# Banded attention with a split-float32 MLP on one core: a longer run of zero matmuls at the start, and the planner's constants set anew

## The chip, the core and the metric

The kernel runs on one core of one Trainium2 chip. Five engines work side by side and wait for one another through semaphores: TensorE (PE in the profile, its weight loads PEld), VectorE (DVE), ScalarE (ACT), GpSimd (POOL) and SyncE (SP, which here issues nearly all transfers). The metric is the device time of one execution in microseconds (us), the median of several executions.

## The reference

Attention for 4 batches and 8 heads, 768 positions of 64 values, then a two-layer MLP on all 3072 tokens. A position sees the first `n_sink` = 4 positions and the last `window` = 128:

```python
keep = is_sink | in_window            # pos < n_sink; 0 <= i - j < window
scores = np.where(keep, q @ k.T / 8, -1e9)
a = softmax(scores)
x = (a @ v) as rows of 512            # 3072 x 512
h = x @ w_in                          # 512 -> 2048
g = h * np.tanh(np.log1p(np.exp(h)))
out = g @ w_out                       # 2048 -> 512
```

The sums are in float64 (the weights arrive as 64-bit numbers); the kernel's products use single precision, each operand of the MLP as a rounded part and a rest.

## The kernel before

The 12 chunks of 256 tokens (`T`) are worked in an order that takes the first chunk of each batch ahead (`c3 == 0`: no earlier keys). For each chunk and each pair of heads there is a score product (L410, or L413 where a chunk has earlier keys), a masked minimum on DVE (L427), an exponential on ACT (L430), transposes on PE (L459, L471) that are copied out of PSUM (`copy_ways`, L271 on ACT or L274 on DVE), and the product with the values (L527). The result x is held as a rounded part (a copy, L271 or L274) and a rest (a subtraction, L282 on POOL or L284 on DVE).

Each of the 16 slices of `w_in` and of `w_out` arrives as 64-bit numbers in a `raw` tile (three of them) and is turned into a rounded part and a rest by `weights`: the high word is scaled (L313 on ACT or L314 on DVE), shifted (L316, DVE) and given its sign (L317, DVE), the low word is scaled (L320 on ACT or L321 on DVE), both are added (L324 on POOL, or line 325 on DVE), then copied (L271, L274) and subtracted (L282, L284).

The MLP goes in steps of two slices. The first product is L584 for the first three chunks, L580 and L581 for the next seven, L642 for the last two, which are worked together; the activation is a chain of five operations between ACT and DVE (L593 to L598, L645 to L650), and the second product is L614 (L668 for the last two chunks). The first three chunks (`GROUP`) are interleaved, two steps each, while their weights are still being turned.

The order of the instructions on every engine is not written by hand. `Plan.solve` puts each operation on one of the engines that can do it, at the time that its own costs and waits give, and `emit` writes the operations by those times. What it weighs are the numbers at the head of the file: ranks (`LEADG` for the attention of the first three chunks, `PACE` between pairs of heads, `WA`, `WB`, `WO` for the weights, `OTF`, `OVF`, `OTP`, `OVP`, `SPL` within a pair), penalties (`PEN_C` for a copy on DVE, `PEN_W` for scaling a weight's word on DVE, `PEN_J` for adding the words on DVE, `PEN_N` for norms on ACT), and the times at which the first loads are planned to land (`EARLY`, `LINE0`). Before `COLD` a PE operation is planned at twice its time. Where the plan leaves PE without work, `emit` fills the hole with matmuls of zeros (L786), 224 columns each.

Ahead of the plan, `body` issues the first eleven loads, computes the masks, and runs `WARM` matmuls of zeros (L1027). After number `AHEAD`, counted from zero, it puts one small matmul (L1032) that spreads the two limits over the partitions. Then every engine reads a flag (L1040) and branches into the planned program.

Of the kernel before, what the change touches and what calls it, by code (L numbers as in the profile page):

```python
# [12 lines left out]
F32 = mybir.dt.float32  # L13
BF16 = mybir.dt.bfloat16
F32R = mybir.dt.float32r
I32 = mybir.dt.int32
# [5 lines left out]
B, H, S, D = 4, 8, 768, 64  # L22
DM, DF = 512, 2048
P = 128
NBLK = S // P
SK = 16
PITCH = P + SK
# [4 lines left out]
TB = 2  # L32
T = TB * P
# [10 lines left out]
       POOL: {PE: 203, ACT: 75, DVE: 80, POOL: 102}, SP: {}}  # L44
W2 = 2 * P + SK
WM = SK + P
PEN_C, PEN_S, PEN_N, PEN_J, PEN_W = 147, 0, 239, 268, 58
OTP, OVP = 1.2, 1
OTF, OVF, PACE = 1.089, 0.601, 1.542
WA, WB, WO = 1.203, -1.766, 0.423  # L50
GROUP, PART, SPARED = 3, 2, 20
PITCHN = 7
LEAD, LEADG, LEADN = 11, (54.195, 35.033, 35.128), 9
WARM, AHEAD, COLD, SPARE, ROOM = 10, 5, 2500, 250, 4
ZERO = 224
SPL = 1.5
LINE0, LINE, SLOW = 8400, 4.5, .2
EARLY = {"ks": ([P, 2 * PITCH], F32, (0, 400, 2400)), "qh": ([P, T], F32, (0, 800, 2700)),
         "vq": ([P, 2, TB, 4, D], F32, (1800, 3900)), "raw": ([P, 512, 2], I32, (4800, 6400, 9300))}
SH, QUICK = 1.0, 2  # L60
HALF = 120
SLACK, STEADY = 800, 24
# [181 lines left out]
class Fast(Base):  # L244
# [9 lines left out]
    def tile(self, b, name):  # L254
        if b.tag in EARLY:
            assert b.place == self.c.order.get(id(b), b.place), "the first loads are out of order"
            b.t = self.c.first[b.tag][b.place]
            return
        n, psum = self.TAGS[b.tag]
        tag, n = (f"{b.tag}{b.place}", 1) if b.tag in ("w", "att") else (b.tag, n)  # L260
        b.t = (self.ps if psum else self.sb).tile(b.shape, b.dtype, name=name, tag=tag, bufs=n)
# [26 lines left out]
    def load(self, prio, buf, dst, src, kb, **kw):  # L288
        if self.c.early.get(buf.tag, 0):
            self.c.early[buf.tag] -= 1  # L290
            k = len(self.c.first[buf.tag]) - self.c.early[buf.tag]
            self.c.order[id(buf)] = k - 1
            return self.plan.add(prio, {SP: (1, lambda: None, EARLY[buf.tag][2][k - 1])}, new=[buf], **kw)
        return self.transfer(prio, dst, src, kb, new=[buf], **kw)
# [58 lines left out]
    def halves(self, b, j0, i0, w, pr, rank):  # L353
# [10 lines left out]
        def twice(buf, t, src, kb):  # L364
            one = self.load(rank, buf, lambda: t()[up], heads(src), kb)
            return [one, self.transfer(rank + .01, lambda: t()[low], heads(src), kb, bufs=[buf])]
        half = lambda: f32(kr.t.rearrange("p n t -> p (n t)")[:, 0:2 * w]).rearrange("p (e w) -> p e w", e=2)
        ldk = twice(kr, half, self.k[b, pr, :, j0 * PITCH:j0 * PITCH + w], w / 2)
        ldq = twice(qr, lambda: qr.t, self.q[b, pr, :, i0 * P:i0 * P + T], T / 2)
        r = rank + SPL  # L370
        k = []
# [616 lines left out]
def body(tc, q, k, v, vs, w_in, w_out, limits, out):  # L988
    nc = tc.nc
    with ExitStack() as ctx:  # L990
        top = ctx.enter_context(tc.tile_pool(name="top", bufs=1))
        held = {tag: [top.tile(shape, dtype, name=f"{tag}{i}") for i in range(Fast.TAGS[tag][0])] for tag, (shape, dtype, _) in EARLY.items()}
        one = top.tile([1, 4], I32, name="lim_one")
# [101 lines left out]
```

## Time and profile before

| | us |
|---|---|
| median of 3 executions | 684.91 (684.52 to 685.14) |
| the profiled execution | 686.47 |
| its span, first to last instruction | 684.7 |
| PE busy | 677.2 (99%) |
| ACT busy, DVE busy, POOL busy | 536.3, 533.5, 153.1 |

The page says that PE is busy 99% of the span, but a matmul that stands and waits is drawn as busy, so this number does not tell where PE works and where it waits. The table of stretches gives more: ACT's busy time of each stretch shows where ACT has no idle left.

### The profile page before, as it was taken

The page shows a single profiled execution, that of the slowest core. Times are in us where ns is not written, and L with a number is a line of the kernel's source. Part 1 is how long each engine was busy: PE and PEld are TensorE (multiplying, and loading weights), DVE is VectorE, ACT ScalarE, POOL GpSimd, SP SyncE. Part 2 cuts the span into 40 slices and gives each one's busy share as a digit, 9 for nine tenths or more (in the row PEclk, how much of TensorE's full clock was granted, in tenths as well). Part 3 has the DMA queues.
Part 4 walks back from the last instruction along what each step waited for, and adds up shares of the span by engine and source line. Part 5 has one row for each costly group of instructions (what it writes and reads, how often), then busy time and mean ns, then how long its engine had stood idle before and what let it go on. Part 6 is the DMA issues. An engine that isn't in the chain of part 4 may idle for free.

```text
span 684.7 us, 13366 instructions
## 1 busy us (share of the span) xinstructions
PE 677.2 (99%) x4642; PEld 573.4 (84%) x4642; DVE 533.5 (78%) x1540; ACT 536.3 (78%) x1219; POOL 153.1 (22%) x144
## 2 busy tenths in 40 slices
PE   9999999999999999999999999999999999999996
PEld 5678888898888888888888888888888888888885
DVE  6998989874798988898899898888988887433333
ACT  5999999887788878777877868986886886656662
POOL 3564333411023223032222124121221210000000
PEclk9999999999999999999999999999999999999998
DMA  7555443421364145053134224234432220000001
GB/s 222 184 187 190 140 162 117 150 66 42 102 176 140 41 144 159 16 173 119 55 114 154 90 75 143 98 96 124 130 96 61 100 73 7 2 32 0 1 0 67
DMA packets 40287, 69.26 MB, mean 101 GB/s; under 512 B 4242, under 2 KB 29074, under 8 KB 40210
## 3 DMA queue, kind: packets, MB, share of 16 engines
q1 hardware_dynamic: 40064, 68.17, 31.8%
q8 instruction: 39, 0.64, 0.4%
q14 instruction: 38, 0.31, 0.1%
q10 hardware_dynamic: 146, 0.13, 0.1%
HBM read 62.00 MB, written 6.29 MB: 100 GB/s over the span
## 4 chain that ended last, share of the span: by engine, by line
PE 95%; ACT 3%; POOL 0%; DVE 0%; issue 0%; DVEq 0%; POOLq 0%
PE acc L614 31%; PE hp L580 15%; PE hp L584 9%; PE hp L581 8%; PE att L527 7%; PE att L413 5%; PE acc L668 3%; PE hp L642 3%; PE att L668 3%; PE att L642 3%; PE att L410 3%; PE att L471 2%; PE att L459 2%; ACT w L271 1%; PE att L508 1%; ACT w L313 1%
## 5 line engine op out<-in xcount | busy, mean ns | idle before, releaser
L614 PE MATMUL acc<-w,gh 128*128 128x512 f32 x640 | 166.0, 396 | 0.0
L580 PE MATMUL hp<-w,w 128*128 128x512 f32 x448 | 163.3, 400 | 0.0
L614 PEld LDWEIGHTS acc<-w,gh 128*128 128x128 f32 x640 | 113.4, 188 | 21.7 <-ACT n L271 0.2
L581 PE MATMUL hp<-w,w 128*128 128x256 f32 x448 | 125.4, 280 | 0.0
L580 PEld LDWEIGHTS hp<-w,w 128*128 128x128 f32 x448 | 84.2, 188 | 17.8 <-DVE n L590 0.3
L430 ACT ACTIVATE p<-p,nm 128x144 f32<-128x144 f32 (+2 forms) x192 | 81.0, 426 | 12.9 <-DVE nm L427 12.0
L282 POOL TENSOR_TENSOR w<-raw,w 64x416 fp32r<-64x416 f32 x41 | 44.2, 1085 | 200.3 <-ACT w L271 59.5
L614 PE MATMUL acc<-w,gl 128*128 128x512 f32 x320 | 87.1, 391 | 0.0
L581 PEld LDWEIGHTS hp<-w,w 128*128 128x128 f32 x448 | 84.5, 189 | 2.0
L590 DVE TENSOR_REDUCE n<-hp 128x256 f32<-128x512 f32 x112 | 76.7, 686 | 10.8 <-PE hp L581 9.5
L584 PE MATMUL hp<-w,w 128*128 128x256 f32 x576 | 77.6, 286 | 0.3 <-DVE u L598 0.2
L584 PEld LDWEIGHTS hp<-w,w 128*128 128x128 f32 x576 | 73.0, 191 | 4.8 <-issue 1.0
L614 PEld LDWEIGHTS acc<-w,gl 128*128 128x128 f32 x320 | 59.7, 188 | 12.8 <-issue 0.2
L271 ACT ACTIVATE gh<-n 128x512 fp32r<-128x512 f32 x69 | 43.5, 631 | 32.5 <-DVE n L598 19.4
L595 ACT ACTIVATE u<-u,bias 128x512 f32<-128x512 f32 x80 | 57.5, 719 | 11.3 <-DVE u L594 10.6
L324 POOL TENSOR_TENSOR w<-w,w 128x512 int32<-128x512 int32 x32 | 41.4, 1303 | 86.6 <-DVE w L316 29.3
L596 ACT ACTIVATE u<-u,bias 128x512 f32<-128x512 f32 x80 | 57.6, 720 | 1.3
L284 DVE TENSOR_TENSOR gl<-n,gh 128x512 fp32r<-128x512 f32 x49 | 34.3, 700 | 27.1 <-PE acc L668 24.0
L598 DVE SCALAR_TENSOR_TENSOR n<-u,n 128x512 f32<-128x512 f32 x56 | 39.7, 710 | 15.5 <-ACT u L597 15.0
L597 ACT ACTIVATE u<-u 128x512 f32<-128x512 f32 x80 | 50.1, 626 | 1.0
L593 ACT ACTIVATE u<-n 128x512 f32<-128x512 f32 x56 | 35.1, 626 | 16.6 <-DVE n L590 14.7
L527 PE MATMUL att<-pth,vq 128*64 128x64 f32 (+2 forms) x1152 | 47.8, 238 | 0.0
(135 smaller groups left out, 1227.6 us busy)
## 6 DMA issues: line engine op xcount, KB each, us to landing
vq<-v_s SPq DMA_DIRECT2D x32, 512.0 KB, 4.0
raw<-k_p SPq DMA_DIRECT2D x64, 208.0 KB, 3.5
raw<-w_in SPq DMA_DIRECT2D x16, 512.0 KB, 3.9
raw<-w_out SPq DMA_DIRECT2D x16, 512.0 KB, 3.9
w<-q_p SPq DMA_DIRECT2D x64, 128.0 KB, 3.1
y<-u SPq DMA_DIRECT2D x20, 256.0 KB, 2.0
ks<-k_p SPq DMA_DIRECT2D x16, 136.0 KB, 3.2
qh<-q_p SPq DMA_DIRECT2D x16, 128.0 KB, 3.0
```

The lines of the kernel that those rows point to most:

```text
L271: ways[ACT] = act_t(n, psum) + more, lambda: nc.scalar.activation(dst(), src(), AF.Copy, scale=scale or 1.0)
L282: ways[POOL] = pool_t(n) + more, lambda: nc.gpsimd.tensor_tensor(dst(), a(), b(), ALU.subtract)
L430: a = add(r + .05 + .01 * e, {ACT: (act_t(n, ptr=2), lambda pv=pv, nm=nm, sm=sm, j=j: nc.scalar.activation(pv(), pv(), AF.Exp, bias=nm.t[: ...
L527: yield nc.tensor.matmul(o.t[e * D:(e + 1) * D, g, o0:o1], w_, pth.t[:, e, c0:c1], start=n_ == 0, stop=n_ == len(jobs) - 1)
L580: yield nc.tensor.matmul(hp.t, wih[f].t[:, fs], xt, start=kt == 0, stop=False)
L581: yield nc.tensor.matmul(hp.t[:, 0, :], wil[f].t[:, fs], xt[:, 0, :], start=False, stop=kt == KT - 1)
L584: yield nc.tensor.matmul(hp.t[:, y, :], w_.t[:, fs], xt[:, z, :], start=kt == 0 and n_ == 0, stop=kt == KT - 1 and n_ == 2)
L590: hs.append(add(r + .3 + .1 * y, {DVE: (dve_t(2 * T), lambda y=y, hp=hp: nc.vector.tensor_reduce(m.t[:, y, :], hp.t.rearrange("p z t -> p ...
L595: a = add(r + .52, {ACT: (act_t(N, ptr=1), lambda: nc.scalar.activation(u.t, u.t, AF.Square, bias=self.one))}, [a], [u])
L596: a = add(r + .53, {ACT: (act_t(N, ptr=1), lambda: nc.scalar.activation(u.t, u.t, AF.Ln, bias=self.half, scale=0.5))}, [a], [u])
L597: a = add(r + .54, {ACT: (act_t(N), lambda: nc.scalar.activation(u.t, u.t, AF.Exp, scale=-1.0))}, [a], [u])
L614: yield nc.tensor.matmul(acc[t].t, g_.t[:, y, ts_], w_.t, start=new and n_ == 0, stop=done)
```

## The change

The zero matmuls ahead of the branch become 15 instead of 10, with the limits' matmul behind the fifth instead of the sixth. The planned landings of the first loads become 400 to 700 ns earlier, the time planned at half speed ends at 2000 instead of 2500 ns, and ranks, penalties and the room rule for the buffers (`ROOM`) get other values.

```diff
-PEN_C, PEN_S, PEN_N, PEN_J, PEN_W = 147, 0, 239, 268, 58
-OTP, OVP = 1.2, 1
-OTF, OVF, PACE = 1.089, 0.601, 1.542
-WA, WB, WO = 1.203, -1.766, 0.423
+PEN_C, PEN_S, PEN_N, PEN_J, PEN_W = 100.000, 0, 283.598, 31.148, 200.107
+OTP, OVP = 1.337, 2.737
+OTF, OVF, PACE = 0.859, 0.242, 0.879
+WA, WB, WO = 0.951, -0.426, 0.866
-LEAD, LEADG, LEADN = 11, (54.195, 35.033, 35.128), 9
-WARM, AHEAD, COLD, SPARE, ROOM = 10, 5, 2500, 250, 4
+LEAD, LEADG, LEADN = 11, (63.148, 36.967, 22.231), 9
+WARM, AHEAD, COLD, SPARE, ROOM = 15, 4, 2000, 250, 2
-SPL = 1.5
-LINE0, LINE, SLOW = 8400, 4.5, .2
+SPL = 0.723
+LINE0, LINE, SLOW = 7700, 4.5, .2
```

(`EARLY` goes the same way: the planned landings of `ks`, `qh`, `vq` and `raw` are 400 to 700 ns earlier, none below zero.)

All products stay; what moves is the order, and which engine does what. Over the whole program the counts change so:

| operation | before | after |
|---|---|---|
| L1027 zero matmuls ahead of the branch, PE | 10 | 15 |
| L786 zero matmuls in the plan's holes, PE | 14 | 37 |
| L313, L314 high word scaled on ACT, on DVE | 27, 5 | 31, 1 |
| L320, L321 low word scaled on ACT, on DVE | 26, 6 | 32, 0 |
| L324, line 325 words added on POOL, on DVE | 32, 0 | 17, 15 |
| L282, L284 rests on POOL, on DVE | 93, 180 | 120, 153 |
| L271, L274 and L273 copies on ACT, on DVE | 353, 60 | 362, 49 |

The start of the planned program on PE. `att` are score and transpose tiles, `ks` and `qh` the keys and queries of a pair of heads, `p` the exponentials, `acc<-zero` a filling matmul. Before:

```order
L410 MATMUL att_0_183<-ks_58,qh_61 128x128
L410 MATMUL att_1_184<-ks_58,qh_61 128x128
L786 LDWEIGHTS zero
L786 MATMUL acc_181<-zero 128x224
L410 MATMUL att_0_188<-ks_58,qh_61 128x256
L410 MATMUL att_1_189<-ks_58,qh_61 128x256
L459 MATMUL att_0_200<-ident,p_14_0_193 128x128 x2
```

And now:

```order
L410 MATMUL att_0_188<-ks_58,qh_61 128x128
L410 MATMUL att_1_189<-ks_58,qh_61 128x128
L786 LDWEIGHTS zero
L786 MATMUL acc_186<-zero 128x224
L410 MATMUL att_0_193<-ks_59,qh_62 128x128
L410 MATMUL att_1_194<-ks_59,qh_62 128x128
L410 MATMUL att_0_205<-ks_58,qh_61 128x256
L410 MATMUL att_1_206<-ks_58,qh_61 128x256
L459 MATMUL att_0_215<-ident,p_14_0_198 128x128 x2
```

The second pair's first scores moved ahead of the first pair's second block and of the first transposes.

The start of the planned program on ACT: `pth` are the transposed exponentials, `raw` a slice of weights, `w` a buffer for weights or x. Before:

```order
L430 ACTIVATE p_14_0_193,sm_2_195<-p_14_0_193,nm_1_194 128x128 x2
L271 ACTIVATE pth_0_205<-att_0_200 128x2x128
L430 ACTIVATE p_14_0_193,sm_2_195<-p_14_0_193,nm_1_194 128x256 x2
L430 ACTIVATE p_28_0_221,sm_2_223<-p_28_0_221,nm_1_222 128x128 x2
L313 ACTIVATE w_0_238<-raw_66 128x512
L271 ACTIVATE pth_0_205<-att_0_229 128x2x256
L430 ACTIVATE p_28_0_221,sm_2_223<-p_28_0_221,nm_1_222 128x256 x2
L271 ACTIVATE n_0_246<-att_0_258 128x256
```

And now:

```order
L430 ACTIVATE p_14_0_198,sm_2_200<-p_14_0_198,nm_1_199 128x128 x2
L430 ACTIVATE p_19_0_209,sm_2_211<-p_19_0_209,nm_1_210 128x128 x2
L271 ACTIVATE pth_0_222<-att_0_215 128x2x128
L430 ACTIVATE p_14_0_198,sm_2_200<-p_14_0_198,nm_1_199 128x256 x2
L271 ACTIVATE pth_0_240<-att_0_233 128x2x128
L320 ACTIVATE w_0_244<-raw_66 128x512
L271 ACTIVATE pth_0_222<-att_0_246 128x2x256
L271 ACTIVATE n_0_265<-rc_0_242 128x256
```

Two exponentials of the second pair moved ahead of the first copy out of PSUM, and a copy more stands ahead of the first work on a weight.

The second activation chain of the MLP on ACT (`u` is its tile, `hp` the first product). Before:

```order
L320 ACTIVATE w_0_962<-raw_68 128x512
L313 ACTIVATE w_0_971<-raw_66 128x512
L593 ACTIVATE u_0_979<-hp_0_749 128x512
L595 ACTIVATE u_0_979<-u_0_979,bias 128x512
L596 ACTIVATE u_0_979<-u_0_979,bias 128x512
```

And now:

```order
L593 ACTIVATE u_0_970<-hp_0_769 128x512
L271 ACTIVATE n_0_952<-att_0_965 128x256
L271 ACTIVATE w_0_981<-w_0_862 128x512
L271 ACTIVATE n_0_991<-rc_0_977 128x256
L271 ACTIVATE pth_0_935<-att_0_984 128x2x256
L271 ACTIVATE w_0_1006<-n_0_952 128x256
L595 ACTIVATE u_0_970<-u_0_970,bias 128x512
```

Five copies came between the chain's first and second operation on ACT, which stood next to each other before.

## Rows read from the trace of the kernel before

**Rows 1.** The profile page's line of busy times (share of the span, instructions).

```profile
PE 677.2 (99%) x4642; PEld 573.4 (84%) x4642; DVE 533.5 (78%) x1540; ACT 536.3 (78%) x1219; POOL 153.1 (22%) x144
```

**Rows 2.** Busy time by stretch: length, each engine's busy us (instructions), granted clock, DMA.

```profile
5.41:16.05 10.64, 10.64 (x49) 6.11 (x51) 5.91 (x30) 7.31 (x27) 2.39 (x3) 1.00 0.76 249
16.05:54.00 37.95, 37.89 (x287) 26.26 (x286) 34.73 (x141) 37.95 (x129) 21.55 (x22) 1.00 0.61 194
54.00:60.00 6.00, 6.00 (x45) 5.06 (x44) 5.04 (x12) 5.44 (x12) 1.75 (x2) 1.00 0.61 190
60.00:106.00 46.00, 45.92 (x298) 39.83 (x298) 41.21 (x102) 45.74 (x96) 17.76 (x14) 1.00 0.46 153
200.00:600.00 400.00, 399.98 (x3005) 345.33 (x3004) 343.50 (x1031) 315.52 (x734) 86.85 (x74) 1.00 0.31 96
```

**Rows 3.** PE in order of time: start, us, line, tiles, shape, [idle before <-releaser].

```profile
1.11 1.30 PE L1027 MATMUL busy<-zero 128*128 128x224 bf16 x6 [1.11 <-DVE zero L1011]
2.34 0.58 PE L1032 MATMUL spread<-lim,ones 1*128 1x2 f32 x2
2.86 0.93 PE L1027 MATMUL busy<-zero 128*128 128x224 bf16 x4
3.91 0.35 PE L786 MATMUL acc<-zero 128*128 128x224 bf16 x1
4.18 0.80 PE L410 MATMUL att<-ks,qh 64*128 64x128 f32 x4
...
6.85 0.58 PE L786 MATMUL acc<-zero 128*128 128x224 bf16 x2
...
12.15 1.55 PE L527 MATMUL att<-pth,vq 128*64 128x256 f32 x8
13.63 1.12 PE L459 MATMUL att<-ident,p 128*128 128x128 f32 x4
...
15.89 0.87 PE L527 MATMUL att<-pth,vq 128*64 128x256 f32 x8
...
17.48 0.66 PE L459 MATMUL att<-ident,p 128*128 128x128 f32 x4
...
24.70 0.35 PE L786 MATMUL acc<-zero 128*128 128x224 bf16 x2
```

**Rows 4.** ACT in order of time, its first operation and its waits up to 16 us.

```profile
5.41 0.40 ACT L430 ACTIVATE p<-p,nm 128x128 f32<-128x128 f32 x1 [2.76 <-DVE nm L427]
...
7.10 0.38 ACT L271 ACTIVATE pth<-att 128x256 f32<-128x256 f32 x1 [0.81 <-PE att L459]
...
10.27 0.66 ACT L313 ACTIVATE w<-raw 128x512 f32<-128x512 f32 x1 [0.86 <-DMA raw<-w_in]
...
14.30 0.42 ACT L271 ACTIVATE w<-n 128x256 fp32r<-128x256 f32 x1 [0.64 <-DVE n L534]
...
16.05 0.38 ACT L271 ACTIVATE n<-att 128x256 f32<-128x256 f32 x1 [0.95 <-PE att L508]
```

**Rows 5.** ACT in order of time, around the second activation chain and behind it.

```profile
56.58 0.60 ACT L593 ACTIVATE u<-hp 128x512 f32<-128x512 f32 x1
57.67 0.73 ACT L595 ACTIVATE u<-u,bias 128x512 f32<-128x512 f32 x1 [0.49 <-DVE u L594]
...
61.63 0.62 ACT L271 ACTIVATE w<-w 128x512 fp32r<-128x512 f32 x1
62.15 0.66 ACT L313 ACTIVATE w<-raw 128x512 f32<-128x512 f32 x1
62.72 0.66 ACT L320 ACTIVATE w<-raw 128x512 int32<-128x512 uint32 x1
63.29 0.71 ACT L595 ACTIVATE u<-u,bias 128x512 f32<-128x512 f32 x1
```

**Rows 6.** POOL and DVE in order of time: the words added, and a DVE operation on 512.

```profile
60.04 1.28 POOL L324 TENSOR_TENSOR w<-w,w 128x512 int32<-128x512 int32 x1 [0.36 <-DVE w L284]
61.46 0.69 DVE L284 TENSOR_TENSOR w<-w,w 128x512 fp32r<-128x512 f32 x1
```

More of the change, by code (lines that the diff above doesn't have):

```diff
@@ L46 @@
 WM = SK + P
-PEN_C, PEN_S, PEN_N, PEN_J, PEN_W = 147, 0, 239, 268, 58
-OTP, OVP = 1.2, 1
-OTF, OVF, PACE = 1.089, 0.601, 1.542
-WA, WB, WO = 1.203, -1.766, 0.423
+PEN_C, PEN_S, PEN_N, PEN_J, PEN_W = 100.000, 0, 283.598, 31.148, 200.107
+OTP, OVP = 1.337, 2.737
+OTF, OVF, PACE = 0.859, 0.242, 0.879
+WA, WB, WO = 0.951, -0.426, 0.866
 GROUP, PART, SPARED = 3, 2, 20
 PITCHN = 7
-LEAD, LEADG, LEADN = 11, (54.195, 35.033, 35.128), 9
-WARM, AHEAD, COLD, SPARE, ROOM = 10, 5, 2500, 250, 4
+LEAD, LEADG, LEADN = 11, (63.148, 36.967, 22.231), 9
+WARM, AHEAD, COLD, SPARE, ROOM = 15, 4, 2000, 250, 2
 ZERO = 224
-SPL = 1.5
-LINE0, LINE, SLOW = 8400, 4.5, .2
-EARLY = {"ks": ([P, 2 * PITCH], F32, (0, 400, 2400)), "qh": ([P, T], F32, (0, 800, 2700)),
-         "vq": ([P, 2, TB, 4, D], F32, (1800, 3900)), "raw": ([P, 512, 2], I32, (4800, 6400, 9300))}
+SPL = 0.723
+LINE0, LINE, SLOW = 7700, 4.5, .2
+EARLY = {"ks": ([P, 2 * PITCH], F32, (0, 0, 1700)), "qh": ([P, T], F32, (0, 100, 2000)),
+         "vq": ([P, 2, TB, 4, D], F32, (1100, 3200)), "raw": ([P, 512, 2], I32, (4100, 5700, 8600))}
 SH, QUICK = 1.0, 2
```

## The prediction

> **What bounds the kernel now.** I read the profile in this order. The page's busy times first [rows 1]: PE is drawn as busy for 677.2 of 684.7 us, but a waiting matmul is drawn as busy, so this only says that PE is never far from the end of the chain. Then the busy times by stretch [rows 2], where the reader should look at ACT. From 16.05 to 54 us ACT is busy 37.95 of 37.95 us, from 60 to 106 us 45.74 of 46. ACT takes its work in order, so there nothing can go faster than ACT does. From 200 to 600 us ACT is busy 315.52 and DVE 343.50 of 400 us, PE 399.98: there PE decides. In between lies a place where the one hands over to the other; I put it at 106 us, since ACT still has hardly any idle up to there. Last the order of time at the start, on PE [rows 3] and on ACT [rows 4]: ACT begins its exponentials at 5.41 us and up to 16.05 us it is idle 10.64 - 7.31 = 3.33 us, nearly all of it in four waits, 0.81 + 0.86 + 0.64 + 0.95 = 3.26 us.
>
> So the time is, in words: when ACT begins, plus ACT's idle, plus ACT's work up to the handover, plus PE's work from there. The change touches the first three. PE's work behind the handover stays: no product is added, and the order there keeps the same pieces.
>
> **ACT's work up to the handover: +3.0 us.** At 106 us the kernel before has done 240 matmuls of the first product (L584) and 98 of the second (L614). The place in the new PE order with the same work left has 246 and 96. I count ACT's instructions up to the one that PE waits for there: 203 before, 209 now. The difference: 17 + 17 scalings of weights (L313, L320) become 21 + 21, the copies of 512 go from 33 to 29, the copies of two times 128 from 9 to 11. A scaling takes 0.57 us from start to start (62.15 to 62.72 to 63.29), a copy of 512 takes 0.52 (61.63 to 62.15) [rows 5]. Drawn times hang over into the next by about 0.10, so a copy of two times 128, drawn with 0.38 [rows 4], counts 0.28. Sum: 8 x 0.57 - 4 x 0.52 + 2 x 0.28 = 4.56 - 2.08 + 0.56 = +3.04 us. The same count at an earlier place (49 us before) gives +1.2, at 60 us +4.1; these are the bounds.
>
> **The start: +1.1 us.** Ahead of the limits' matmul one zero matmul falls away; it costs nothing either way, since that matmul waits for DVE's limits. Behind it stand ten instead of four, and the first scores follow them on PE. Six take 1.30 us and four 0.93 [rows 3], so one more costs 0.185, six more 1.11 us; were the clock already up, two take 0.35 instead of 0.58, and it would be 0.67. The scores' operands don't hide this: the first scores started right behind the zeros, at 4.18. The first exponential, 1.23 us behind them, comes at about 6.5.
>
> **ACT's idle up to 16 us: -1.7 us.** TensorE runs at its low level at first. The granted clock is drawn as 1.00 throughout [rows 2], but eight matmuls of L527 take 1.55 us at 12.15 and 0.87 at 15.89, four transposes 1.12 at 13.63 and 0.66 at 17.48 [rows 3]: between lies the step from 1.2 to 2.4 GHz, at about 15 us. Before it PE had stood with gaps between zero matmuls, scores and transposes. Now 37 instead of 14 filling matmuls close gaps, 23 of them more within about the first 35 us, so I expect the step some microseconds earlier. The four waits then: the wait for the first transposes (0.81) now has two exponentials of the second pair in it, whose scores come late too: 0.5 left. The wait for the first weights (0.86) vanishes, since ACT starts later and has a copy more ahead of them. The last two (0.64 + 0.95 = 1.59) are PE's chain at the low level; at the high one L527 and the transposes give back 0.68 + 0.46 = 1.14, 0.45 left. Against this stands the run of five zero matmuls ahead of the second transposes, 0.93 us if it still falls in the low level: I count 0.7 for it. Left 0.5 + 0 + 0.45 + 0.7 = 1.65, gained 3.33 - 1.65 = 1.7. The bounds are 3.3 (no wait is left) and 0.1 lost (0.9 off for the weights, five and six zero matmuls, 11 x 0.09, on).
>
> The Trainium skill (page "TensorE: Matmul & The Clock Gate", Part 1, "What's actually happening") says that the low level is the default and that activity lifts it, at a place that moves from run to run of the same kernel. By that rule this term differs between executions; the three timed ones of before lie within 0.62 us, so the trace bears the rule out only as far as that, and the sum above does without it.
>
> **ACT's idle at 54 to 60 us: -0.5 us.** ACT is busy 5.44 of 6.00 us there [rows 2]; 0.49 of the hole is the wait between the first and second operation of the second activation chain [rows 5], which stand next to each other. Now five copies lie between, more than the wait. Other chains could open a hole elsewhere; none stands next to its successor in the new order before the handover, so I count nothing for that.
>
> **The words added on DVE, not on POOL: 0 on the path.** Fifteen additions (L324, 1.28 us on POOL [rows 6]) go to DVE, six of them before the handover. The trace has no such operation on DVE. It goes over 1024 half words; the nearest row is an operation on 512 words at 0.69 us [rows 6], so I bound it by 0.69 and 1.38, and take 0.69 to 1.0, six at 4 to 6 us. DVE's idle covers it: it was busy 34.73 of 37.95 and 41.21 of 46 us [rows 2], 8 us idle. At 1.38 each, 8.3 us, the cover is gone.
>
> The Trainium skill (page "VectorE: DVE Perf Modes", "Walkthrough: the 8-slice pipeline in each mode") gives one result a cycle at 0.96 GHz, or two for packed 16-bit operands: an estimate from that page is 1.07 or 0.53 us. By either the cover holds and the sum stays; no run here shows it yet.
>
> **The rest.** The loads keep their own order until the branch; `EARLY`, `LINE0` and `COLD` only tell the plan when to expect them. The stage from 200 us on stays on PE with DVE idle 56 of 400 us and ACT 84, so POOL's 27 added subtractions are hidden there.
>
> **The sum.** +3.0 + 1.1 - 1.7 - 0.5 = +1.9 us. The profiled execution took 686.47 us (span 684.70 and 1.77 around it) and would take 688.4; the median of the runs is 684.91, 1.6 lower, and I carry the difference over: 686.8 us.
>
> **The rivals.**
> 1. The start pays for ACT's extra work. If the clock rises before the first transposes, all 3.3 us of waits go: 3.0 + 1.1 - 3.3 - 0.5 = +0.3, 685.2 us. For it speaks that nearly all the waits sit in PE's chain; against it that ACT starts 1.1 us later and cannot win back what it has not begun. It decides once the waits left are under 0.5 us.
> 2. ACT's longer path doesn't count. If the place that decides is the earlier one, where ACT has only 1.2 us more, and the clock is up within the zero matmuls: 1.2 + 0.67 - 3.3 - 0.5 = -1.9, 683.0 us, faster. For it: the excess swings from 1.2 to 4.1 along the way. Against it: ACT's 45.74 of 46 us up to the handover.
> 3. DVE becomes the bound: the six additions at 1.38 us or more eat its idle, and its copies come late for ACT. The price is what exceeds the 8 us, with the 5 us of other work that also moved: about 2 us on top, 688.8 us. It decides from 1.3 us an addition.
> 4. The change doesn't do what it says: the clock doesn't rise earlier, since scores still wait between the zero matmuls, and every filling matmul costs 0.185. Then 3.0 + 1.1 + 0.1 = +4.2, 689.1 us.
>
> **How the numbers follow.** The forecast, 686.8 with a range of its own of 685.7 to 688.3, has 0.39; rival 1 has 0.25, rival 2 0.17, rival 3 0.09, rival 4 0.10. The predicted time is the forecast's. A measurement of this kernel can tell about 0.2%, 1.4 us, from no change. Faster (under 683.5): rival 2, 0.17. Same (683.5 to 686.3): rival 1 and the lower edge of the forecast, 0.25 + 0.08 = 0.33. Slower: the rest, 0.50. The range that leaves out 2 in 10 drops half of rival 2 below and most of rival 4 above: 683.1 to 689.2 us.
>
> **What the new profile would show.** PE's first scores at 5.3 instead of 4.18 us, the first exponential at 6.5 instead of 5.41: the start is right. The step in the durations of L527 or the transposes before 12 us: the clock's term is right; still at 15 us, rival 4. ACT's idle from its first exponential to 16 us at 1.7 us: the third term. ACT full to about 110 us or longer, and the 97th matmul of L614 at about 108 us instead of 106: ACT's extra work counts. If ACT shows idle from 60 to 106 us, then not ACT but PE or DVE decided there, and the first term is wrong. DVE full in that stretch, with line 325 over 1.3 us: rival 3.

## The result, and the profile after

The changed kernel takes 688.93 us (median of 3 runs, 688.21 to 689.64) against 684.91 before: 1.0057 times as long, interval 1.0043 to 1.0071, or 4.0 us. The forecast was 686.8 us, within 683.1 to 689.2, and slower. The sign held. The range held too, but only just: 688.9 lies 0.3 us under its upper end and outside the 685.7 to 688.3 that the forecast had for itself. The number came out 2.1 us short.

The profiled execution of after took 689.64 us with a span of 687.8, that of before 686.47 with 684.7: 3.1 to 3.2 us between the two profiles, 4.0 between the medians, since before's profiled execution lay 1.6 us over its median and after's 0.7. So both profiles show executions that are slower than the middle one, and this will matter for the waits near the start.

First the page's line of busy times, as [rows 1].

```profile
PE 677.6 (99%) x4670; PEld 575.1 (84%) x4670; DVE 515.3 (75%) x1508; ACT 541.2 (79%) x1237; POOL 169.4 (25%) x158
```

Then the stretches of [rows 2], with the same columns: stretch, length, busy us of PE, PEld, DVE, ACT and POOL (instructions), granted clock, DMA share, GB/s.

```profile
5.41:16.05 10.64, 8.17 (x57) 5.35 (x55) 5.77 (x28) 7.34 (x28) 1.28 (x1) 0.95 0.73 253
16.05:54.00 37.95, 37.76 (x281) 25.49 (x277) 32.37 (x133) 37.26 (x122) 18.37 (x21) 0.97 0.58 179
54.00:60.00 6.00, 6.00 (x48) 4.86 (x47) 4.74 (x17) 5.86 (x19) 2.73 (x3) 1.00 0.77 220
60.00:106.00 46.00, 45.60 (x301) 40.02 (x299) 42.85 (x106) 46.00 (x98) 14.08 (x11) 1.00 0.44 151
200.00:600.00 400.00, 400.00 (x3005) 345.81 (x3005) 326.81 (x993) 316.10 (x747) 117.42 (x98) 1.00 0.32 97
```

ACT is again full from 60 to 106 us, and PE again full from 200 us on. The first line is the one that differs most: PE was busy for 10.64 of 10.64 us before and is now for 8.17. PE in order of time, as [rows 3], shows the hole.

```profile
5.08 0.49 PE L410 MATMUL att<-ks,qh 64*128 64x128 f32 x4
...
9.90 0.70 PE L410 MATMUL att<-ks,qh 64*128 64x256 f32 x2
13.06 0.70 PE L410 MATMUL att<-ks,qh 64*128 64x256 f32 x2 [2.47 <-DVE nm L427]
...
16.79 1.06 PE L459 MATMUL att<-ident,p 128*128 128x128 f32 x4
...
18.81 0.87 PE L527 MATMUL att<-pth,vq 128*64 128x256 f32 x8
```

The first scores run at the high level already (0.49 us for four, 0.80 in [rows 3]); behind the hole the transposes take 1.06 us for four, which is the low level again (0.66 at the high one). The granted clock by stretch says the same, columns as above:

```profile
10.00:14.90 4.90, 2.43 (x15) 1.22 (x15) 2.86 (x14) 3.03 (x9) 1.28 (x1) 1.00 0.53 196
14.90:18.30 3.40, 3.40 (x17) 2.08 (x15) 2.66 (x10) 3.08 (x11) 0.73 (x1) 0.50 0.70 214
18.30:30.00 11.70, 11.59 (x95) 8.12 (x92) 10.73 (x46) 11.33 (x39) 3.91 (x5) 1.00 0.58 185
```

What PE waited for stands on ACT and DVE. ACT in order of time, its first operation and its waits, as [rows 4]:

```profile
6.00 0.40 ACT L430 ACTIVATE p<-p,nm 128x128 f32<-128x128 f32 x1 [3.35 <-DVE nm L427]
...
11.12 0.68 ACT L320 ACTIVATE w<-raw 128x512 int32<-128x512 uint32 x1 [1.95 <-DMA raw<-w_in]
...
12.85 0.42 ACT L271 ACTIVATE n<-rc 128x256 f32<-128x256 f32 x1 [0.58 <-DVE rc L439]
...
17.29 0.41 ACT L271 ACTIVATE n<-rc 128x256 f32<-128x256 f32 x1 [0.32 <-DVE rc L439]
...
18.93 0.40 ACT L430 ACTIVATE p<-p,nm 128x128 f32<-128x128 f32 x1 [0.25 <-DVE nm L427]
```

And DVE in order of time over the same place:

```profile
11.12 0.43 DVE L314 TENSOR_SCALAR w<-raw 128x512 f32<-128x512 f32 x1 [3.65 <-DMA raw<-w_in]
11.58 0.43 DVE L316 TENSOR_SCALAR w<-w 128x512 int32<-128x512 int32 x1
...
12.04 0.69 DVE L317 SCALAR_TENSOR_TENSOR w<-raw,w 128x512 int32<-128x512 int32 x1
...
12.74 0.26 DVE L427 CUSTOM_DVE_ANT_0 p<-att,m 128x128 f32<-128x128 f32 x1
```

The first weight slice lands at 11.1 us in this execution. In the new order both engines have an operation on it standing in line: DVE from 7.5 us (3.65 us of wait), ACT from 9.2 us (1.95). Everything behind it on DVE, the masking of scores (L427) among it, waits as well, and so PE waits for L427 until 13.06.

The words added on DVE, the operation that no row of before had, from the instructions of line 325 (count: shortest, median, longest in ns, first and last start in us):

```profile
L325 DVE CUSTOM_DVE_ANT_0 w<-w,w x15: 666/680/694, 50.7 to 140.8; 128x1024 uint16<-128x1024 uint16 x15
```

### The profile page after: what moved, and what is told of

Same layout as the page of the kernel before. It is cut to its first block, busy times and chain, and to the rows that moved or that the text cites. A ratio compares the mean times of both kernels' runs of the same rounds, so it can differ in the third digit from the quotient of the medians.

```text
span 687.8 us, 13484 instructions
## 1 busy us (share of the span) xinstructions
PE 677.6 (99%) x4670; PEld 575.1 (84%) x4670; DVE 515.3 (75%) x1508; ACT 541.2 (79%) x1237; POOL 169.4 (25%) x158
## 4 chain that ended last, share of the span: by engine, by line
PE 91%; ACT 5%; DMA 1%; DVE 1%; SPq 1%; issue 0%
PE acc L614 31%; PE hp L580 15%; PE hp L584 8%; PE hp L581 8%; PE att L527 6%; PE att L413 5%; PE hp L642 3%; PE att L642 3%; PE att L668 3%; PE acc L668 3%; PE att L471 2%; PE att L410 1%; ACT p L430 1%; PE att L459 1%; DMA raw<-w_in 1%; ACT w L271 1%
## 5 line engine op out<-in xcount | busy, mean ns | idle before, releaser
L614 PE MATMUL acc<-w,gh 128*128 128x512 f32 x640 | 163.0, 396 | 0.0
L614 PEld LDWEIGHTS acc<-w,gh 128*128 128x128 f32 x640 | 114.6, 188 | 23.1 <-ACT u L593 0.2
L614 PE MATMUL acc<-w,gl 128*128 128x512 f32 x320 | 88.5, 392 | 0.0
L282 POOL TENSOR_TENSOR gl<-n,gh 128x512 fp32r<-128x512 f32 x37 | 47.8, 1292 | 164.7 <-ACT gh L271 91.1
L584 PE MATMUL hp<-w,w 128*128 128x256 f32 x576 | 77.9, 286 | 0.4 <-DVE u L598 0.3
L584 PEld LDWEIGHTS hp<-w,w 128*128 128x128 f32 x576 | 73.0, 190 | 5.0 <-issue 1.8
L282 POOL TENSOR_TENSOR w<-raw,w 64x416 fp32r<-64x416 f32 x44 | 47.5, 1085 | 99.7 <-ACT w L271 57.4
L614 PEld LDWEIGHTS acc<-w,gl 128*128 128x128 f32 x320 | 59.7, 188 | 12.2 <-issue 0.2
L271 ACT ACTIVATE gh<-n 128x512 fp32r<-128x512 f32 x66 | 41.6, 631 | 35.0 <-DVE n L598 17.7
L282 POOL TENSOR_TENSOR w<-w,w 128x512 fp32r<-128x512 f32 x30 | 38.7, 1290 | 80.4 <-ACT w L271 19.4
L594 DVE TENSOR_SCALAR u<-u 128x512 f32<-128x512 f32 x80 | 41.9, 524 | 7.8 <-ACT u L593 7.1
```

The source lines that it names most:

```text
L271: ways[ACT] = act_t(n, psum) + more, lambda: nc.scalar.activation(dst(), src(), AF.Copy, scale=scale or 1.0)
L282: ways[POOL] = pool_t(n) + more, lambda: nc.gpsimd.tensor_tensor(dst(), a(), b(), ALU.subtract)
L584: yield nc.tensor.matmul(hp.t[:, y, :], w_.t[:, fs], xt[:, z, :], start=kt == 0 and n_ == 0, stop=kt == KT - 1 and n_ == 2)
L594: a = add(r + .51, {DVE: shared((dve_t(N, True), lambda: nc.vector.tensor_scalar(u.t, u.t, E20, None, ALU.min)))}, [a], [u])
L614: yield nc.tensor.matmul(acc[t].t, g_.t[:, y, ts_], w_.t, start=new and n_ == 0, stop=done)
```

## The theories

Theory 1 is the prediction's own: up to the handover at about 106 us ACT is the bound, so the time is ACT's start plus its waits plus the sum of its work, and the new order has 3.0 us more of that work. Theory 2: the hole and the clock that falls behind it make the loss by 19 us, and ACT's work later on doesn't matter. Theory 3 came up after the first runs: DVE's queue is the bound there. Rival 4, in the expectations of the third group of runs, is that the weight scalings which the new PEN constants gave to ACT are the loss by themselves. All ratios are to runs of the kernel before on the same chip; its median was 684.88 to 685.24 us in all of them. The edits are shown shortened: long lines are broken, and lines that only keep count, or give a lambda its arguments, are left out.

## Taking work from ACT, and giving it some

**Eight scalings to VectorE, in after and in before.** The plan stays as solved; of ACT's weight scalings (s1, s4) the 9th to 16th are issued on DVE where they stand.

```diff
-            n0 = len(nc.cur_bb.bb.instructions)
+            n0, here = len(nc.cur_bb.bb.instructions), t.eng == ACT and t in self.scalings
+            self.scaled += here
+            t.eng = DVE if here and 9 <= self.scaled <= 16 else t.eng
```

> The kernel after, with the 9th to 16th of the weight scalings that its plan gave to ScalarE (four of L313, four of L320) done by VectorE at the same places; the start and the early hole are untouched. ScalarE has 8 x 0.57 = 4.6 us less up to the handover; VectorE has about 4 x 0.6 + 4 x 0.7 us more, with room (it was busy for 45.85 of the 49 us from 60 us on, 32.42 of 38 before it, so part of it may show). Theory 1: 3.0 to 4.6 us less than the kernel after, or 1.5 if VectorE's queue takes half back: 684.3 to 687.4. Theory 2: within 0.5 us of the kernel after (688.9), since the loss has been made by 19 us.

> The kernel before with the same edit: the 9th to 16th of its ScalarE weight scalings done by VectorE at the same places. Theory 1: ScalarE is the bound up to the handover here too, so 1.5 to 4 us less than the kernel before, 680.9 to 683.4, which would be under both kernels. Theory 2: nothing, 684.4 to 685.4; more if VectorE is filled up: up to 687.

Measured: after with the edit 690.10 us, ratio 1.0063 (1.0047 to 1.0079), no less than after's 1.0057. Before with the edit 687.35, ratio 1.0036 (1.0023 to 1.0049): 2.5 us slower, where theory 1 had expected a gain, although a scaling takes 0.41 us on DVE where I had counted 0.6 to 0.7. ACT is indeed emptied, but it then stands and waits. Before with the edit, ACT in order of time:

```profile
55.61 0.60 ACT L593 ACTIVATE u<-hp 128x512 f32<-128x512 f32 x1 [0.98 <-PE hp L584]
57.98 0.72 ACT L595 ACTIVATE u<-u,bias 128x512 f32<-128x512 f32 x1 [1.77 <-DVE u L594]
```

The same kernel, DVE in order of time:

```profile
55.25 0.41 DVE L321 TENSOR_SCALAR w<-raw 128x512 int32<-128x512 uint32 x1
55.59 0.41 DVE L316 TENSOR_SCALAR w<-w 128x512 int32<-128x512 int32 x1
55.92 0.42 DVE L314 TENSOR_SCALAR w<-raw 128x512 f32<-128x512 f32 x1
56.26 0.41 DVE L321 TENSOR_SCALAR w<-raw 128x512 int32<-128x512 uint32 x1
56.59 0.68 DVE L317 SCALAR_TENSOR_TENSOR w<-raw,w 128x512 int32<-128x512 int32 x1
57.20 0.41 DVE L316 TENSOR_SCALAR w<-w 128x512 int32<-128x512 int32 x1
57.53 0.41 DVE L594 TENSOR_SCALAR u<-u 128x512 f32<-128x512 f32 x1
```

DVE works without a gap, and L594, for which ACT's activation chain waits 1.77 us, stands behind the scalings that were put there. So a little work moved from ACT to DVE makes DVE the late one: the plan before left no room for it at that place. These two runs don't decide between theories 1 and 3, since both say that the receiver can be the next bound. After with the edit had no stretch at the low level behind its hole and was no faster, which speaks against theory 2's clock, but only as a hint, since the edit by itself cost 2.5 us in before.

**Eight scalings to GpSimd.** The same eight, issued on POOL.

```diff
+            self.pooled[s1] = lambda: nc.gpsimd.tensor_scalar(f32(z.t), f32(hw()), 2.0 ** -112, None, ALU.mult)
-            r = t.ways[t.eng][1]()
+            r = self.pooled[t]() if here and 9 <= self.scaled <= 16 else t.ways[t.eng][1]()
```

> The kernel after, with the 9th to 16th of its ScalarE weight scalings (four of L313, four of L320, the ones that went to VectorE in the run before) done by GpSimd at the same places. ScalarE has 8 x 0.57 = 4.6 us less, VectorE no more than before, GpSimd about 8 x 1.2 us more, where it was busy for 14 of 49 us. Theory 1 (ScalarE's work up to the handover is the bound): 3 to 4.6 us less than the kernel after, 684.3 to 685.9. Theory 2 (the loss is made by 19 us): within 0.5 us of the kernel after. Theory 3 (VectorE's queue is the bound up to the handover, since 4.6 us more on it cost both kernels time): within 0.5 us, or up to 1.5 us more where GpSimd hands the scaled words to VectorE later.

> The kernel before with the same edit as in the kernel after: its 9th to 16th ScalarE weight scalings done by GpSimd at the same places, where GpSimd was busy for 18 of 49 us. Theory 1: 2 to 4 us less than the kernel before, 680.9 to 682.9, under both kernels. Theories 2 and 3: within 0.5 us, or more if GpSimd's queue is filled up.

Measured: 700.47 us (ratio 1.0220, 1.0196 to 1.0244) and 692.54 (1.0102, 1.0082 to 1.0122), far slower, as no theory had said. I had put a scaling on POOL at 1.2 us. Before with the edit, the scalings on POOL, by line (columns as for line 325):

```profile
L315 POOL TENSOR_SCALAR w<-raw x4: 1511/1576/1972, 54.3 to 67.4; 128x512 f32<-128x512 f32 x4
```

and ACT in order of time there:

```profile
60.06 0.72 ACT L595 ACTIVATE u<-u,bias 128x512 f32<-128x512 f32 x1 [4.88 <-DVE u L594]
```

A scaling takes about 1.6 us on POOL, DVE's shift (L316) waits for it with the rest of DVE's queue behind it, and ACT waits 4.88 us for DVE. This says nothing on ACT's work; it says that ACT, DVE and POOL hand the weights on in fixed order and that any of them can be made the late one. So no run here takes work from ACT without loading another engine; ACT's share is shown by giving it work.

**Eight scalings twice.** To give ACT work and touch nothing else, before with the same eight done twice.

```diff
-                chain(n0)
+                chain(n0); n0 = len(nc.cur_bb.bb.instructions)
+                here and 9 <= self.scaled <= 16 and (t.ways[ACT][1](), chain(n0))
```

> The kernel before, with the 9th to 16th of its ScalarE weight scalings done twice in a row, with the same operands: 8 x 0.57 = 4.6 us more ScalarE work up to the handover and nothing else, half as much again as the change adds. Theory 1: 3 to 4.6 us more than the kernel before, 687.9 to 689.5. Theories 2 and 3: no more than 0.5 us, since ScalarE's work there is not the bound.

Measured: 691.40 us, ratio 1.0090 (1.0070 to 1.0110), 6.5 us more where I had counted 4.6 us of work. Theories 2 and 3 had said 0.5 at most; both fall for the kernel before. Its stretch from 60 to 106 us, columns as above:

```profile
60.00:106.00 46.00, 41.91 (x261) 36.61 (x261) 36.80 (x92) 45.00 (x95) 15.76 (x13) 0.96 0.40 135
```

and PE in order of time in it:

```profile
61.53 0.98 PE L584 MATMUL hp<-w,w 128*128 128x256 f32 x6 [1.43 <-DVE u L598]
...
70.49 2.90 PE L584 MATMUL hp<-w,w 128*128 128x256 f32 x12 [2.57 <-DVE u L598]
```

ACT is busy for 45.00 of the 46 us while PE and DVE (36.80 of 46 us, 41.21 in [rows 2]) go idle behind it. After the hole of 2.57 us the granted clock falls (0.96 on average, and twelve matmuls of L584 take 2.90 us where the next twelve, at 76.26 us, take 1.59 at the high level). Most of the price is ACT's work all the same, for a scaling done twice costs more than two of them. ACT in order of time:

```profile
62.70 1.37 ACT L313 ACTIVATE w<-raw 128x512 f32<-128x512 f32 x2
63.98 1.38 ACT L320 ACTIVATE w<-raw 128x512 int32<-128x512 uint32 x2
65.25 0.72 ACT L595 ACTIVATE u<-u,bias 128x512 f32<-128x512 f32 x1
```

A pair takes 1.27 to 1.28 us from start to start, where one takes 0.57. The stretch from ACT's first operation to the 99th matmul of L614, the place of the handover in before, columns as above:

```profile
5.40:110.39 104.99, 99.98 (x673) 77.39 (x674) 86.37 (x283) 101.63 (x270) 43.42 (x40) 0.98 0.53 173
```

ACT is busy for 101.63 us there, against 96.42 in before: 5.2 of the 6.5 us. Whether the fall of the clock has a part in the rest is not shown.

## Changing the plan's constants

**The PEN constants, each way.** These are the penalties by which the plan gives work to DVE; the plan is solved anew with one line changed.

```diff
-PEN_C, PEN_S, PEN_N, PEN_J, PEN_W = 100.000, 0, 283.598, 31.148, 200.107
+PEN_C, PEN_S, PEN_N, PEN_J, PEN_W = 147, 0, 239, 268, 58
```

> The kernel after with the five PEN constants of the kernel before; the plan is solved anew. Up to the first 150 rows of ScalarE's order it has 20 weight scalings (29 in the kernel after, 23 in the one before), but more copies (L271: 70, against 59 and 64), so that ScalarE's work ahead of the handover, counted with the durations of the trace of before, comes out 0.3 us above the kernel after and 3.3 above the one before. Theory 1 (the sum of ScalarE's work counts, whatever it consists of): 688 to 690, as the kernel after. Rival 4 (the scalings that the new constants gave to ScalarE are the loss): back to the kernel before, 684.5 to 686.

> The kernel before with the five PEN constants of the kernel after alone; the plan is solved anew. ScalarE's work ahead of the handover, counted with the durations of the trace of before, grows by 6.9 us (31 scalings in the first 150 rows where there were 23). Theory 1: 5.5 to 7.5 us more than the kernel before, 690.4 to 692.4. Rival 4 (the constants cost what they cost in the kernel after): 3 to 4.5 us more, 688 to 689.4. Theory 2 (the hole by 15 us): no more than 1 us.

Measured: after with the old constants 689.56 us, ratio 1.0066 (1.0050 to 1.0082); before with the new ones 690.79, ratio 1.0079 (1.0065 to 1.0093), 5.6 us more. In both the time came out within theory 1's bounds, which went by the sum of ACT's work, and not within rival 4's, which went by the number of scalings. In the first, ACT gave fourteen of its 63 scalings to DVE and got more copies instead (L271: 381, 362 in after); the sum was counted at 3.3 us above before, and the loss is 4.3. Its trace agrees: up to the place with as many matmul columns left as at before's handover, ACT is busy for 99.77 us, 3.35 more than before's 96.42. In the second the sum was counted at 6.9 us more, and 5.6 came out, at the lower end of what theory 1 allowed. Here the trace agrees only in part: up to that place ACT is busy for 100.42 us, 4.0 more, and the stretch behind it takes 580.6 us, 1.9 longer than before's, for which I have no explanation. Rival 4 falls by both.

## The start, and the first weights

**The zero matmuls alone.** Before with the new start:

```diff
-WARM, AHEAD, COLD, SPARE, ROOM = 10, 5, 2500, 250, 4
+WARM, AHEAD, COLD, SPARE, ROOM = 15, 4, 2500, 250, 4
```

> The kernel before, with WARM and AHEAD alone set to 15 and 4: six zero matmuls more ahead of the first scores, the plan and its order otherwise as before. ScalarE's work up to the handover stays as in the kernel before. Theory 1 (the 3.0 us of extra ScalarE work up to the handover are the loss): this kernel loses only its later first exp (+0.6 us, as in the kernel after) and gains the waits of [rows 4] that a clock up by 5 us shortens (up to 1.5 us of the 3.3): -0.9 to +0.6 us against the kernel before, so 684.0 to 685.5. Theory 2 (the hole in TensorE at 10 to 15 us and the clock that falls after it are the loss): the earlier clock brings TensorE to the first weights before they have landed, as in the kernel after, so a stretch at the half clock after 13 us and +1.5 to +3.5 us: 686.4 to 688.4.

Measured: 685.47 us, ratio 1.0006 (0.9994 to 1.0019), within theory 1's bounds and under theory 2's. ACT begins at 6.58 us in place of 5.41, 1.2 us later, as the prediction had it (1.1). Only 0.6 us of that shows in the median, since ACT waits less behind the later start: it idles 1.05 us from its first operation to 16.05 us. The low level lasted to 10.5 us in this execution.

**The first slice's work, later.** After, with the five operations on the first weight slice issued just ahead of that slice's rounding copy.

```diff
-        self.emit(self.plan.solve())
+        done, own = self.plan.solve(), self.slice0[:5]
+        self.emit([x for t in done if t not in own
+                   for x in ((*(z for z in done if z in own), t) if t is self.slice0[5] else (t,))])
```

> The kernel after, with the five instructions that read the first weight slice (L314, L316, L317 on VectorE, L320 on ScalarE, L324 on GpSimd) moved behind, to just ahead of that slice's rounding copy, so that neither ScalarE nor VectorE stands in line for the load that lands at 11.1 us; ScalarE's amount of work is the same. Theory 2: the hole of 2.47 us in TensorE and the half clock from 14.9 to 18.3 us go, and with them 2.0 to 3.4 us: 685.5 to 686.9. Theory 1: only ScalarE's own wait of 1.95 us goes, and what of it ScalarE does not wait for later is gained: 0 to 2.0 us, and the kernel stays above the one before by the rest of its extra work, 687.0 to 688.9.

**The first slice's work, on something else.** After, with these operations reading a query tile.

```diff
-            hw = lambda raw=raw: raw.t[:, :, 1]
+            hw = lambda: qh0[:, None, :].to_broadcast([P, 2, T])   # first slice only
```

> The kernel after, with the four instructions that read the first weight slice (L314, L317 on VectorE, L320 on ScalarE) reading a query tile that has long landed in place of the load that lands at 11.1 us; that one slice is thereby left out of the result. The waits of 3.65 us on VectorE and 1.95 us on ScalarE for that load go, and with them the hole of 2.47 us in TensorE. Theory 2: 2.0 to 3.4 us less than the kernel after, 685.5 to 686.9. Theory 1: ScalarE gets up to 1.95 us back, so 0 to 2.0 less, 687.0 to 688.9. Theory 3: VectorE gets 3.65 us back, of which at most the hole counts: 1 to 2.5 less.

Measured: 694.39 us (1.0131, 1.0114 to 1.0149) and 693.54 (1.0114, 1.0093 to 1.0136). Neither did what it was for. In both, another load had been issued into the buffer that they read by the time they came up in the order: the buffer of the first slice held a later slice by then (so that slice's part of the result is that of another), the query tile the next chunk. So they waited for that load, to 14.64 and 13.54 us. After with the query tile, ACT in order of time:

```profile
13.54 0.63 ACT L320 ACTIVATE w<-qh 128x512 int32<-128x512 uint32 x1 [2.76 <-DMA qh<-q_p]
```

What they measure is therefore the opposite: the operations on the first slice starting 3.5 and 2.4 us later cost 5.5 and 4.6 us against after. The price is over one for one; the clock was low for longer too (granted 0.93 from 16.05 to 54 us in the second, 0.97 in after).

**The first weights, sooner.** After, with that load issued ahead of the two first value loads.

```diff
         for pr in range(3):
             nc.sync.dma_start(held["ks"][pr][:, 0:w], k[0, pr, :, 0:w])
             nc.sync.dma_start(held["qh"][pr], q[0, pr, :, 0:T])
-            if pr:
-                nc.sync.dma_start(fronts(held["vq"][pr - 1]), ...)
+        nc.sync.dma_start(held["raw"][0].rearrange("p n t -> p (n t)"), w_in[0].bitcast(I32))
+        for pr in range(2):
+            nc.sync.dma_start(fronts(held["vq"][pr]), ...)
```

> The kernel after, with the first weight load issued ahead of the two first value loads, so 0.9 us sooner and with 256 KB less ahead of it; the value loads land later, but are wanted only at 14 us. The first weights should land at 9.3 to 10.2 us in place of 11.1. ScalarE waits for them from 9.2 us on, VectorE from 7.5 us. Theory 1: the wait of 1.95 us shrinks by the 0.9 to 1.8 us, and all of it counts, since ScalarE is the bound behind it: 686.9 to 688.2. Theory 2: the hole shrinks by as much and the clock may hold, so 1.0 to 3.4 us less: 685.5 to 687.9. Nothing, 688.5 to 689.5, if the load lands no earlier for being issued earlier, or if ScalarE then waits for the values instead.

Measured: 687.59 us, ratio 1.0034 (1.0023 to 1.0045), 1.3 us under after's median, or 1.7 when each is compared with before on its own chip (4.0 and 2.35 us over it). DVE in order of time:

```profile
9.24 0.43 DVE L314 TENSOR_SCALAR w<-raw 128x512 f32<-128x512 f32 x1 [0.57 <-DMA raw<-w_in]
```

and ACT:

```profile
6.40 0.40 ACT L430 ACTIVATE p<-p,nm 128x128 f32<-128x128 f32 x1 [3.75 <-DVE nm L427]
...
10.70 0.66 ACT L320 ACTIVATE w<-raw 128x512 int32<-128x512 uint32 x1
```

The slice lands at 9.2 us, 1.9 earlier than in after's profile; ACT no longer waits for it, and PE has no hole and no second stretch at the low level. So wait, hole and fall of the clock together are not the whole loss: 2.4 us stay, with ACT full to 106 us as before, and theory 2 falls for after too. What the early load won, 1.3 to 1.7 us, is at the edge of what these runs tell apart, since the intervals of the two ratios just touch.

**One execution, or the kernel.** Some of the runs above are further executions of the same start. After with eight scalings on DVE and on POOL keeps after's order up to 32 us; before with eight on DVE, on POOL, or done twice keeps before's up to 51 us. Their stretch up to 16.05 us: before with eight done twice, then after with eight on DVE, then on POOL, columns as above.

```profile
5.41:16.05 10.64, 9.93 (x65) 5.92 (x66) 7.58 (x37) 9.08 (x34) 2.36 (x3) 1.00 0.86 281
5.41:16.05 10.64, 9.65 (x61) 6.01 (x62) 5.94 (x29) 7.81 (x28) 1.27 (x1) 1.00 0.81 258
5.41:16.05 10.64, 10.27 (x68) 6.56 (x68) 6.68 (x33) 8.46 (x30) 1.71 (x2) 1.00 0.87 278
```

With before's start ACT idles 10.64 - 9.08 = 1.6 us here (1.8 and 1.5 in the other two), where [rows 2] has 3.3. With after's start, where ACT begins at 6.39 and 6.37 us, it idles 1.9 and 1.2 us, where after's profile has 2.7. ACT's wait for the first weights in after with eight on DVE:

```profile
10.98 0.68 ACT L320 ACTIVATE w<-raw 128x512 int32<-128x512 uint32 x1 [0.75 <-DMA raw<-w_in]
```

With eight on POOL the slice lands at 10.25 us and ACT does not wait for it at all; PE's hole is 0.99 and 0.37 us in these two, and no stretch at the low level follows it. So the wait of 1.95 us, the hole of 2.47 and the fall of the clock belong to after's profiled execution, as the four waits of [rows 4] in their full length belong to before's.

**The same edit in before.**

> The kernel before, with the same move of the first weight load ahead of the two first value loads. Its ScalarE waits only 0.86 us for that load [rows 4], not 1.95. Theory 1 (what ScalarE gets back of a wait is what the time gets back, and no more): 0 to 0.9 us less than the kernel before, 684.0 to 684.9, the fastest of all if anything. If the gain of 1.3 us that the move gave the kernel after came from the early load as such (TensorE, the clock) and not from the length of ScalarE's wait, 1.0 to 1.5 us less: 683.4 to 683.9. More than the kernel before if the value loads, now later, are waited for.

Measured: 684.37 us against 685.20, ratio 0.9987 (0.9979 to 0.9996). The gain of 0.8 us is no more than ACT's wait for that load (0.86 in [rows 4], 0.83, 0.55 and 0.52 in the three further executions of before's start), as theory 1 had it, and this is the fastest kernel of all, though by less than the 0.2% that I would call a difference. It also makes a clean pair with the last run: in neither does ACT wait for the first weights. The stretch up to 16.05 us of after with the early load:

```profile
5.41:16.05 10.64, 10.64 (x64) 6.98 (x64) 6.47 (x32) 8.00 (x29) 1.39 (x2) 1.00 0.86 274
```

and of before with it:

```profile
5.41:16.05 10.64, 10.61 (x66) 6.42 (x66) 7.54 (x39) 9.43 (x35) 2.36 (x3) 1.00 0.87 286
```

ACT has 1.43 us less behind it in the first: 0.99 of that is the later start (6.40 against 5.41), 0.44 more waiting. At 54 to 60 us it has 0.5 back (5.86 against 5.36 busy). The two spans differ by 686.7 - 682.7 = 4.0, the medians by 3.2.

## Why the prediction held, and where it was short

The prediction's sum can be taken term by term from a pair of traces: ACT's start, its work and its idle up to the handover (the 99th matmul of L614 in before's order, the 97th in after's), and the stretch behind it. Before and after as first profiled, then before and after with the early load, from ACT's first operation to the handover, columns as above:

```profile
5.41:105.99 100.58, 100.44 (x672) 77.26 (x673) 86.87 (x283) 96.42 (x262) 43.44 (x40) 1.00 0.56 181
6.00:108.89 102.89, 99.83 (x698) 77.77 (x695) 88.22 (x286) 99.35 (x268) 36.45 (x35) 0.98 0.53 174
5.41:103.86 98.45, 98.30 (x672) 76.16 (x673) 86.78 (x283) 96.44 (x262) 43.44 (x40) 1.00 0.58 185
6.40:107.43 101.03, 100.32 (x697) 78.45 (x698) 88.08 (x286) 99.12 (x268) 36.43 (x35) 1.00 0.58 178
```

| us, after less before | start | ACT's work | ACT's idle | behind | sum |
|---|---|---|---|---|---|
| foretold | +1.1 | +3.0 | -1.7 - 0.5 | 0 | +1.9 |
| as first profiled | +0.59 | +2.93 | -0.62 | +0.20 | +3.1 |
| with the early load | +0.99 | +2.68 | -0.10 | +0.43 | +4.0 |

Start and work came out nearly as foretold, and the idle did not: of the 2.2 us that were to be won there, 0.6 and 0.1 were. (These are the profiled executions. The medians differ by 4.0 and 3.2 us; after with the early load was profiled 0.8 us above its median.)

- **What bounds the kernel: right.** ACT is full up to the handover in both kernels, and the stretch behind it takes 578.7 to 579.3 us in all four traces. Giving work to ACT alone in before cost at least that work. For after itself this is read from the traces and not shown by a run of its own.
- **ACT's work, +3.0 us: right, as the later place has it.** It measures 2.9 and 2.7. The 97th matmul of L614, foretold for 108 us, starts at 108.9; the place with the same work left in before was at 106.0. Rival 2, which went by the earlier place, falls.
- **The start, +1.1: right in size.** First scores at 5.08 us (5.3 foretold) and first exponential at 6.00 in the profile of after, whose clock rose unusually early; in the runs with the low level up to 8.7 us or later it is 6.4 to 6.6.
- **ACT's idle up to 16 us, -1.7: this step failed.** In the profile of after ACT idles 10.05 - 7.34 = 2.7 us from its first operation to 16.05 us instead of 3.33, and between 16.05 and 54 us another 0.69 appears, so nothing is left of the gain. In the further executions of both starts it idles 1.9 and 1.2 us, against 1.8, 1.6 and 1.5 for before: there was no gain to be had. What was wrong first is that four waits of one execution were read as the kernel's; 1.5 to 1.8 of the 3.3 us were that execution's own, which was also 1.6 us above its median. Second, "the wait for the first weights (0.86) vanishes, since ACT starts later and has a copy more ahead of them" holds in one of three executions only: the wait is 1.95, 0.75 and nothing. I had moved ACT's start by the zero matmuls but not pulled its work forward by the faster clock that the same paragraph counted on. In after's profile TensorE was quick, ACT came to the weights at 9.2 us, and the load landed at 11.1; it landed at 11.0 and 10.3 in the two others, where TensorE was slower. So the landing did not come sooner when the engines did, and their lead turned into waiting.
- **The step of the clock: not the change's doing.** The prediction took the 23 extra fillers in the first 35 us to bring the step forward. The profiles since say that it moves without them. By the durations of scores and transposes the low level ended between 8.6 and 10.7 us in five runs with before's ten zero matmuls, and at 15 us only in the one profiled execution that I had; with fifteen it ended between 8.7 and 11.9 us in seven runs, and before 5 us only in after's profile. So it came no earlier with the change. This is the condition of rival 4, whose 689.1 us lies nearest to the measured 688.9; but rival 4 leaves out the 0.5 us at 54 us (with it, 688.6), and it has no wait for weights. That the measured time fell inside the range at all is owed to the room that the range left for rival 4.
- **Idle at 54 to 60 us, -0.5: right** (5.86 busy in place of 5.44).
- **The words added on DVE, 0 on the path: right.** 0.68 us each, at the lower bound, and rival 3 falls. The cover that I named, 8 us of DVE's idle, is thinner than its sum: eight small scalings at one place were enough to make ACT wait for DVE.

The Trainium skill (page "TensorE: Matmul & The Clock Gate", Part 1, "What's actually happening") says that the place of the step differs between runs of one kernel. The traces now agree: the low level ended at about 9 to 15 us in four executions of before's start, and at under 5 to about 9 us in three of after's. I had set that rule aside for the sum, since the timed runs lay so close together; it should have kept me from reading four waits of a single execution as the kernel's.

## What to carry to other kernels

Where one engine with a fixed order is full up to a handover, count its whole work up to there by kind and duration; that sum forecast two re-solved plans within 1.4 us (in one of them with a part that came from behind the handover), while the number of scalings did not. Then take each transfer that an early operation needs and ask when each engine now reaches that operation: where the load lands no sooner, an engine that arrives sooner waits longer, and all that is queued behind it waits too. Before a gain is booked on the waits near a program's start, compare them over several executions.

## What was unexpected on the chip

- TensorE's level rose at very different times in executions of the same start, from about 9 to 15 us in before's, and it fell again after holes of 2.5 us (after, at 14.9 us; before with eight scalings twice, at 70.5 us), each time for some microseconds.
- A multiplication by a constant on 128x512 takes about 1.6 us on GpSimd (1.51 to 1.97), 0.41 to 0.43 on VectorE and 0.57 on ScalarE from start to start. I had expected 1.2 on GpSimd, from its addition of two tiles at 1.28.
- The addition of 1024 half words (L325) takes 0.68 us on VectorE, as long as an operation on 512 words [rows 6]. The Trainium skill (page "VectorE: DVE Perf Modes", "Walkthrough: the 8-slice pipeline in each mode") gives one or two results a cycle, from which I had estimated 1.07 or 0.53 us; the measurement lies nearer the estimate at two results a cycle.
